# A longer opening run of zeros on TensorE, a later spread of norm's factors, and the first decays in two transfers and scans

## The chip, the cores and the metric

The kernel runs on one core of a Trainium2 chip. The metric is the device time of one execution in microseconds (us), and the median of several runs is compared. The engines are named as in the profile: PE (TensorE's matmuls; PEld are its weight loads), DVE (VectorE), ACT (ScalarE), POOL (GpSimd) and SP (SyncE, which here issues the DMA transfers). They run side by side and wait for each other by semaphores; each of them executes its own instructions strictly in the order of the program.

## What is computed

A gated linear attention over 4 batches x 8 heads x 768 steps with head size 48, and then a normed, gated feed-forward layer on its 3072 tokens of 384 features:

```python
state = alpha[:, :, t, :, None] * state + np.einsum('bhd,bhe->bhde', k[:, :, t], v[:, :, t])
y[:, :, t] = np.einsum('bhd,bhde->bhe', q[:, :, t], state)
...
rms = np.sqrt(np.mean(x * x, axis=-1, keepdims=True) + 1e-06)
xn = x / rms * rms_g
g = xn @ w_gate
silu = g * (1.0 / (1.0 + np.exp(-g)))
val = xn @ w_val
return (silu * val @ w_out).astype(np.float32)
```

The weights of the feed-forward layer come as 64-bit floats (w_gate and w_val 384 x 1536, w_out 1536 x 384).

## The kernel before, in words

**Chunks.** The 768 steps of each batch are cut into 6 chunks of 128 steps, all heads together, so that there are 24 chunks of 128 tokens. `attention(cc)` records the work of chunk cc. Chunks 0 to 3 are the first of their batches (`first`), have no state before them, and are computed with 32-bit matmuls; the others use 16-bit matmuls with each number split into a high and a low part.

**One first chunk, step by step.** SP loads the block `att` of the chunk: the decays (522 columns), then q and k (1024 columns). For chunks 0 and 1 these are two transfers (`cuts`), for the others one. DVE runs two scans over the 520 decay columns (`scan`, L661: cumulated products, four head pairs and two halves of the chunk in one row, each of these 8 segments starting anew), the first forward, the second backward from the reciprocals of the first one's ends (`turn`, L681). DVE multiplies q and k by the results (`mul_q` L698, `mul_k` L691). PE turns k (`k_across`, L893), computes the scores (`scores`, L778), DVE masks them (`masked32`, L794), and PE multiplies by v (`output32`, L804). The state goes through L908 on PE, two copies on ACT and L813 on PE. ACT squares the output (`square`, L960), POOL makes the norm's root, DVE multiplies by the root and by the factors rms_g (`scaled`, L974), and PE turns the result (`x_across` L981, with a low part by L995).

**The factors.** rms_g is loaded as one row (`load_rg`, L626), spread to all 128 partitions by a matmul with a row of ones, `unit` (`rg_wide`, L632), and copied back by ACT (`rg_take`, L635). `unit` lies in the same buffer as `junk`, the zeros that PE multiplies.

**The feed-forward layer.** Each of 18 weight tiles is loaded, folded and put together by ACT and DVE (`decode`: L536 on ACT, L541 and L544 on DVE, L502 on ACT, L552 on DVE). The chunks form groups of 4, 2, 2, 4, 4, 4 and 4. For each group and each of 12 weight tiles, PE runs two banks of 9 matmuls (L1149), ACT takes a silu of the first bank (L1160), DVE multiplies it with the second (L1166), and ACT and DVE split the product (L502, L1179). The second layer follows (L1219). In group 0, the first 5 weight tiles are run for chunks 0 and 1, and then for 2 and 3.

**What sets the order.** Nothing is issued by hand: `Plan.op` records each piece of work with its engine, a cost in us, what it depends on and which buffers it uses. `Plan.order` gives each piece a due time, from those of its users and from the tables `GAP`, `DUE`, `LATE` and `W_LATE`, and then lays the pieces out on a model of the five engines; the program's order on each engine is the result. Any cost or table entry that changes can so change the order of everything behind it. Where the model finds PE idle before its 45th microsecond, it fills in multiplications of a constant tile (`warm`, L1329), as many as fit at 0.24 us each.

**PE's start.** `warm_first` (L621) is PE's first piece: 14 matmuls of zeros, planned as 4.8 us.

```python
for _ in range(WARM_FIRST):
    nc.tensor.matmul(ps[:, :DM], junk[:, :P], junk, start=True, stop=True)
...
op("PE", 4.8, warm_first, [], [("mm", "warm")])
```

Of the kernel before, what the change touches and what calls it, by code (L numbers as in the profile page):

```python
# [8 lines left out]
F32 = mybir.dt.float32  # L9
# [37 lines left out]
GROUPS = [4, 2, 2, 4, 4, 4, 4]  # L47
EARLY = 5


# [10 lines left out]
COST = dict(  # L61
    scan=1.16, rec=0.18, kh=0.6, qh=0.33, kl=0.6, vl=0.47, ql=0.62, gd=0.12, sd=0.28, sl=0.27, mask=0.59,
    al=0.59, st=0.27, ss=0.12, x=0.46, xl=0.47, shift=0.53, rest=0.88, wl=0.87, ob=0.46,
# [12 lines left out]
PACE = [1.0, 1.0, 1.15, 1.18, 1.18, 1.18, 1.18]  # L76
GAP = [-15.7, 137.0, 36.9, 106.2, -22.7, -134.2, 399.9]
DUE = [
    -719.9, -428.4, 411.3, -551.6, 184.4, 443.0, 1038.8, 186.9, 211.3, 740.5, 1018.7, 654.7, 756.4,
    831.8, 770.0, 432.6, 1179.9, 1019.1, 1109.0, 512.2, 336.7, 338.7, 475.6, 483.2,  # L80
]
LATE = dict(
    a16=95.7, abs=95.5, add=-3.0, al=-37.8, cnt=239.3, dec=-143.8, gd=128.7, k16=-225.5, kb=-100.3,
    kh=211.5, kl=37.3, kp=-148.6, ld2=204.9, load=96.2, mask=-127.2, near=132.3, ob=-144.7,
    odd=-153.0, pow=73.9, q16=-96.0, qh=38.4, ql=-11.4, rec=52.2, rest=-69.8, rg=8.7, rgt=-201.8,
    rgw=-6.4, s16=44.3, sc=-125.2, sc32=-36.5, scan=303.9, sd=70.9, shift=-71.0, sl=-52.1, sq=109.6,
    st=-82.7, st0=-193.5, take=-59.8, u=-107.2, u32=-53.5, v=186.2, v16=124.3, vl=-14.9, wh=160.7,
    wid=-93.7, wl=-301.4, wl2=15.7, wneg=80.9, x=-230.4, x16=-36.5, x32=-16.4, xb=-7.0, xl=-43.5,
    xneg=126.0, xp=27.6, y32=-52.5, ys=-23.6, ys32=-78.8, ysw=-43.9, yv=-74.0, yvw=-116.3,
)  # L90
LATE_CHECK = 3
W_LATE = [
    -285.5, -492.0, -249.7, -250.4, -99.8, -149.6, -106.2, -73.2, 53.8, -132.7, 151.4, 126.2, 126.8,
    172.8, 286.5, 195.7, 182.1, 333.3,
]
WARM_UNTIL, WARM, WARM_FIRST = 45.0, 0.24, 14
CUTS = [0, 2, 4]
# [3 lines left out]
class Plan:  # L101
# [9 lines left out]
    def op(self, engine, cost, fn, deps=(), use=(), due=None, lock=False, kb=0, late=0.0, kind=None, tile=None):  # L111

        o = dict(e=engine, c=cost, fn=fn, d=[d for d in deps if d], u=tuple(use), due=due, lock=lock,
                 kb=kb, late=late, i=len(self.ops), n=[], k=kind, w=tile)
        for d in o["d"]:
            d["n"].append(o)
        for k in o["u"]:
            self.users[k] = self.users.get(k, 0) + 1
        self.ops.append(o)
        return o  # L120
# [224 lines left out]
def tile_attn_moe(  # L345
# [12 lines left out]
    nc = tc.nc  # L358
# [70 lines left out]


    tab = const.tile([1, 1], F32, name="tab")
    nc.gpsimd.memset(tab, 0.0)
    nc.scalar.activation(tab, tab, AF.Silu)
    rg = const.tile([P, DM], F32, name="rg")


    junk = const.tile([P, DM], mybir.dt.bfloat16, name="junk")
    unit = junk.bitcast(F32)[:1, :P]
    nc.vector.memset(junk, 0.0)
    nc.vector.memset(unit, 1.0)  # L440
    seed = const.tile([R, 2, NP, HC + 1], F32, name="seed")
# [71 lines left out]
    def add(engine, kind, *args, **kw):  # L513
        w = kw.get("tile")
        late = LATE.get(kind, 0.0) + (W_LATE[w] if w is not None else 0.0)
        return op(engine, COST[kind], *args, late=late, kind=kind, **kw)
# [105 lines left out]

    op("PE", 4.8, warm_first, [], [("mm", "warm")])

# [12 lines left out]
    def attention(cc):  # L637
# [18 lines left out]

        def scan(back, start):
            x, w = att_tile(cc)[:R, :o_a], decays()[:, o_f:]
            if back:
                x, w = [y[:R, 1 : o_a + 1][:, ::-1] for y in (att_tile(cc), decays())]  # L660
            nc.vector.tensor_tensor_scan(  # L661
                w, x, start.rearrange("r g p c -> r (g p c)"), 0.0, op0=ALU.mult, op1=ALU.add
            )
# [358 lines left out]
        att_k, w_k, at0, at1 = key("att"), key("w"), ("at", (cc, 0)), ("at", (cc, 1))  # L1022
        cuts = ((0, o_q), (o_q, AW)) if cc < 2 else ((0, AW),)
        la = [
# [6 lines left out]
        if cc == 0:  # L1031
            x = op("SP", 0.45, load_rg, kb=20, kind="rg", late=LATE.get("rg", 0.0))
            y = add("PE", "rgw", rg_wide, [x], [("mm", "rg")])
            tiles["rg"] = add("ACT", "rgt", rg_take, [y], [("mm", "rg")])
        before = state_ops.get(cc - NB, {})
        prev = state_ops.get(cc - 1, {})
        s1 = add("DVE", "scan", lambda: scan(False, seed), [la[0]], [att_k, w_k], lock=True)
        rec = add("DVE", "rec", turn, [s1, prev.get("s2")], [w_k])
# [10 lines left out]
        if first:  # L1049
# [4 lines left out]
            k_k, u_k = ("at", (cc, 4)), ("at", (cc, 2))  # L1054
            kt = add("PE", "kp", k_across, [kh], [key("kh"), k_k])
            kt = add("ACT", "kb", k_back, [kt], [key("kT"), k_k])
            y0 = add("PE", "y32", output32, [m, lv], [key("a16"), key("v"), key("y")])
# [25 lines left out]
        if cc in WIDE:  # L1083
            y_k = key("x32")
            y1 = add("ACT", "take", take, [y1], [key("y"), y_k])
            y1 = add("DVE", "add", add_up, [y1], [key("y"), y_k])
        sq = add("ACT", "sq", square, [y1], [y_k])
        rt = add("POOL", "pow", root, [sq], [key("ss")], lock=True)
# [422 lines left out]
```

## Time and profile before

| | before |
|---|---|
| median of 3 runs | 514.42 us (514.36, 514.42, 516.57) |
| the profiled execution | 516.7 us |
| its span, first to last instruction | 514.9 us |
| busy, share of the span | PE 98%, DVE 75%, PEld 59%, ACT 49%, POOL 6% |
| first gate matmul (L1149) on PE | 34.62 us after the start |
| last matmul's end | 510.9 us |
| moved from and to HBM | 52.03 MB read, 4.72 MB written |

How to read it: a row of the timeline gives the start, the duration, the engine, the line, the operation with its tiles and shapes, how many instructions were merged, and in brackets how long the engine idled before it and what ended that. "busy" of PE counts from the start of a matmul to its modelled end, so PE can be busy with work that is of no use to the result, such as multiplied zeros, or with work that runs slowly. In the table of stretches, each engine has its busy time and, in brackets, how many instructions; then come the granted clock, the share of the DMA engines' time, and GB/s.

### The profile page before, as it was taken

To read this page: it belongs to the slowest core of one execution; us is meant where nothing else is said; L and a number is where in the kernel's file an instruction comes from. 1 tells how busy PE (TensorE), PEld (TensorE's weight loads), DVE (VectorE), ACT (ScalarE), POOL (GpSimd) and SP (SyncE) were. 2 spreads that over 40 slices of the span, in tenths; PEclk is the share of its full clock that TensorE was granted. 3 is DMA by queue.
4 is the path that set the end of the run, shared out by engine and by line. 5 is a ranking of instruction groups with operands and counts; after the bars stand their busy time and mean duration, and the time that the engine had idled before them with its cause. 6 is when DMAs were issued, how large, how long until landed. Compare 5 with 4: busy or idle time off the path is not lost.

```text
span 514.9 us, 12237 instructions
## 1 busy us (share of the span) xinstructions
PE 507.0 (98%) x5004; PEld 302.5 (59%) x5004; DVE 387.0 (75%) x734; ACT 254.1 (49%) x669; POOL 30.0 (6%) x85
## 2 busy tenths in 40 slices
PE   8999999999999999999999999999999999999996
PEld 4687844668877886445556545556544456444453
DVE  6999999999999999969999998995364320233321
ACT  2578977635644762448644356754365310233300
POOL 4011000100000100001111000100010000000000
PEclk9999999999999999999999999999999999999999
DMA  8979866566542645321675824018862000000001
GB/s 295 297 229 263 226 220 212 154 124 165 114 96 94 130 116 138 96 81 32 142 229 149 179 89 168 17 32 277 287 203 77 1 17 31 17 0 1 0 31 36
DMA packets 64031, 65.19 MB, mean 127 GB/s; under 512 B 32993, under 2 KB 57570, under 8 KB 63970
## 3 DMA queue, kind: packets, MB, share of 16 engines
q1 hardware_dynamic: 63970, 64.36, 44.5%
q8 instruction: 40, 0.66, 0.5%
q14 instruction: 21, 0.17, 0.1%
HBM read 52.03 MB, written 4.72 MB: 110 GB/s over the span
## 4 chain that ended last, share of the span: by engine, by line
PE 87%; DVE 5%; issue 1%; ACT 1%; DVEq 0%; ACTq 0%
PE mm L1149 53%; PE mm_po L1219 25%; PE at L768 3%; PE y L856 2%; PE at L933 1%; PE y L835 1%; DVE w L661 1%; DVE wu_i L544 0%; DVE wg L552 0%; DVE wu_i L541 0%; DVE qp L698 0%; DVE k L705 0%; DVE kh L691 0%; ACT h L502 0%; DVE h L1166 0%
## 5 line engine op out<-in xcount | busy, mean ns | idle before, releaser
L1149 PE MATMUL mm<-xT,wg 128*128 128x512 f16 (+1 forms) x1602 | 287.5, 338 | 0.0
L1149 PEld LDWEIGHTS <-wg 128*128 128x128 f16 x1602 | 153.8, 98 | 120.0 <-issue 0.5
L1219 PE MATMUL mm_po<-wo,h 128*128 128x384 f16 x864 | 144.0, 326 | 0.0
L1219 PEld LDWEIGHTS <-h 128*128 128x128 f16 x864 | 83.2, 98 | 55.8 <-issue 1.0
L1166 DVE SCALAR_TENSOR_TENSOR h<-mm,sl 128x512 f32<-128x512 f32 (+1 forms) x89 | 51.6, 584 | 46.0 <-PE mm L1149 43.4
L502 ACT ACTIVATE h<-h 128x512 f16<-128x512 f32 (+1 forms) x89 | 48.6, 546 | 73.5 <-DVE h L1166 73.0
L1160 ACT ACTIVATE sl<-mm 128x512 f32<-128x512 f32 (+1 forms) x89 | 45.5, 511 | 49.1 <-PE mm L1149 48.0
L1179 DVE TENSOR_TENSOR h<-h,h 128x512 f16<-128x512 f32 (+1 forms) x89 | 51.5, 584 | 18.1 <-ACT h L502 18.1
L661 DVE TENSOR_TENSOR_SCAN w<-att,seed 112x520 f32<-112x520 f32 x48 | 59.4, 1238 | 2.5 <-DMA att<-att 1.8
L1230 DVE TENSOR_SCALAR ob<-mm_po 128x384 f32<-128x384 f32 x24 | 13.2, 553 | 34.3 <-PE mm_po L1219 34.2
L964 POOL TENSOR_TENSOR ss<-ssq,eps 128x1 f32<-128x1 f32 x24 | 10.2, 425 | 351.8 <-ACT junk L960 351.8
L883 ACT CAST a<-at 128x512 f16<-128x512 f32 x40 | 22.9, 584 | 15.6 <-DVE at L784 15.5
L784 DVE TENSOR_TENSOR at<-at,mask 128x512 f32<-128x512 f32 x40 | 26.2, 690 | 2.3 <-PE at L768 2.1
L886 DVE TENSOR_TENSOR a<-at,a 128x512 f16<-128x512 f32 x40 | 26.4, 681 | 0.0
L502 ACT ACTIVATE q<-qp 112x512 f16<-112x512 f32 x20 | 12.5, 627 | 18.1 <-DVE qp L698 17.0
L698 DVE TENSOR_TENSOR qp<-att,w 112x256 f32<-112x256 f32 x48 | 18.8, 419 | 0.1
L768 PEld LDWEIGHTS <-k 48*128 48x128 f16 x480 | 13.5, 94 | 6.6 <-issue 5.1
L768 PE MATMUL at<-q,k 48*128 48x128 f16 x480 | 17.1, 217 | 0.1
L502 ACT ACTIVATION_READ_ACCUMULATOR h<-h 128x1 f32 x89 | 16.7, 188 | 0.0
L691 DVE TENSOR_TENSOR kh<-att,w 112x512 f32<-112x512 f32 x24 | 16.4, 684 | 0.0
L684 ACT COPY dec<-w 112x8 f32<-112x8 f32 x24 | 4.9, 203 | 22.3 <-DVE w L661 22.1
L608 ACT ACTIVATE wu_c<-wu_c 128x768 f32<-128x768 f32 x12 | 10.0, 836 | 9.4 <-DVE wu_c L602 9.4
(134 smaller groups left out, 449.3 us busy)
## 6 DMA issues: line engine op xcount, KB each, us to landing
att<-att SPq DMA_DIRECT2D x22, 773.0 KB, 5.1
v<-vtok SPq DMA_DIRECT2D x24, 192.0 KB, 3.1
out_dram<-ob SPq DMA_DIRECT2D x24, 192.0 KB, 2.0
raw_c<-w_gate SPq DMA_DIRECT2D x12, 384.0 KB, 4.1
raw_c<-w_val SPq DMA_DIRECT2D x12, 384.0 KB, 5.0
raw_d<-w_out SPq DMA_DIRECT2D x6, 768.0 KB, 4.5
raw_i<-w_gate SPq DMA_DIRECT2D x11, 384.0 KB, 4.3
raw_i<-w_val SPq DMA_DIRECT2D x11, 384.0 KB, 5.0
```

Source lines behind the costliest of these rows:

```text
L502: nc.scalar.activation(dst, src, AF.Copy, scale=scale, accum_out=stat[:rows, col : col + 1])
L661: nc.vector.tensor_tensor_scan(w, x, start.rearrange("r g p c -> r (g p c)"), 0.0, op0=ALU.mult, op1=ALU.add)
L698: nc.vector.tensor_tensor(by_half(t["qp"])[:, g], q, w, op=ALU.mult)
L768: nc.tensor.matmul(t["sc"][j][:, p, :], t["k16"][r, x, p, :], t["q16"][r, y, p, :], start=m == 0, stop=m == 2,)
L784: nc.vector.tensor_tensor(t["sc"][j], t["sc"][j], mask.to_broadcast([P, NP, C]), op=ALU.mult)
L883: nc.scalar.copy(a_tile()[:, j, 0], t["sc"][j])
L886: nc.vector.tensor_tensor(a_tile()[:, j, 1], t["sc"][j], a_tile()[:, j, 0], op=ALU.subtract)
L1149: nc.tensor.matmul(ps[:, :n], wg[:, f, x, j, kk, :], xT[:, y, kk, cs], start=i == 0, stop=i == 3 * NK - 1,)
L1160: nc.scalar.activation(t["sl"][:, :n], t[0][:, :n], AF.Silu, scale=1.0 / (S_X * S_W))
L1166: nc.vector.scalar_tensor_tensor(t["h"][:, :n], t[1][:, :n], S_H / (S_X * S_W), t["sl"][:, :n], op0=ALU.mult, op1=ALU.mult,)
L1179: nc.vector.tensor_tensor(h16_of(g, f)[:, 1, cs], t["h"][:, :n], h16_of(g, f)[:, 0, cs], op=ALU.subtract)
L1219: nc.tensor.matmul(t[i][:, :DM], h16_of(g, f)[:, x, ts], wo[:, f // 2, y, f % 2, :], start=f == 0 and m == 0, stop=f == NF - 1 and m == 2,)
```

## The change

The diff without the new numbers of the planner's tables (`GAP`, `DUE`, `LATE` and `W_LATE` are all replaced, which moves work on every engine):

```diff
+HALVED = 1
...
-    scan=1.16, rec=0.18, kh=0.6, qh=0.33, kl=0.6, vl=0.47, ql=0.62, gd=0.12, sd=0.28, sl=0.27, mask=0.59,
+    scan=1.16, half=0.62, rec=0.18, kh=0.6, qh=0.33, kl=0.6, vl=0.47, ql=0.62, gd=0.12, sd=0.28, sl=0.27, mask=0.59,
...
-WARM_UNTIL, WARM, WARM_FIRST = 45.0, 0.24, 14
+WARM_UNTIL, WARM, WARM_FIRST, WARM_COST = 45.0, 0.24, 21, 7.9
...
+    junk = const.tile([P, DM], mybir.dt.bfloat16, name="junk")
+    nc.vector.memset(junk, 0.0)
     tab = const.tile([1, 1], F32, name="tab")
...
-    junk = const.tile([P, DM], mybir.dt.bfloat16, name="junk")
-    unit = junk.bitcast(F32)[:1, :P]
-    nc.vector.memset(junk, 0.0)
-    nc.vector.memset(unit, 1.0)
+    unit = const.tile([1, P], F32, name="unit")
+    nc.gpsimd.memset(unit, 1.0)
...
-    op("PE", 4.8, warm_first, [], [("mm", "warm")])
+    op("SP", 0.8, lambda: None, due=-1000.0)
+    op("PE", WARM_COST, warm_first, [], [("mm", "warm")])
...
-        def scan(back, start):
+        def scan(back, start, lo=0, hi=o_a):
...
             nc.vector.tensor_tensor_scan(
-                w, x, start.rearrange("r g p c -> r (g p c)"), 0.0, op0=ALU.mult, op1=ALU.add
+                w[:, lo:hi], x[:, lo:hi], start.rearrange("r g p c -> r (g p c)")[:, lo:hi], 0.0,
+                op0=ALU.mult, op1=ALU.add,
             )
...
-        cuts = ((0, o_q), (o_q, AW)) if cc < 2 else ((0, AW),)
+        at = [0] + ([SEG] if cc < HALVED else []) + ([o_q] if cc < 2 else []) + [AW]
+        cuts = list(zip(at, at[1:]))
...
-            y = add("PE", "rgw", rg_wide, [x], [("mm", "rg")])
-            tiles["rg"] = add("ACT", "rgt", rg_take, [y], [("mm", "rg")])
+            lrg = x
...
-        s1 = add("DVE", "scan", lambda: scan(False, seed), [la[0]], [att_k, w_k], lock=True)
+        if cc < HALVED:
+            s1 = None
+            for x, lo, hi in ((la[0], 0, SEG), (la[1], SEG, o_a)):
+                s1 = op("DVE", COST["half"], lambda lo=lo, hi=hi: scan(False, seed, lo, hi), [x, s1], [att_k, w_k],
+                        lock=True, late=LATE.get("scan", 0.0), kind="scan")
+        else:
+            s1 = add("DVE", "scan", lambda: scan(False, seed), [la[0]], [att_k, w_k], lock=True)
...
+            if cc == 0:
+                y = add("PE", "rgw", rg_wide, [lrg, kt, sc], [("mm", "rg")])
+                tiles["rg"] = add("ACT", "rgt", rg_take, [y], [("mm", "rg")])
...
-        sq = add("ACT", "sq", square, [y1], [y_k])
+        sq = add("ACT", "sq", square, [y1, tiles["rg"]], [y_k])
```

So there are four parts. The zeros of `junk` are the first instruction on DVE and `unit` has a tile of its own; PE multiplies zeros 21 times, planned as 7.9 us. `rg_wide` depends on chunk 0's turned k and scores, and the squares depend on the factors. Chunk 0's decay block comes in two transfers of 260 and 262 columns, with a forward scan for each. And the tables are new. The dummy piece on SP delays nothing on the chip: it has no instruction, and stands only in the planner's model.

What the new order looks like where it matters. First PE, from the last multiplied zeros to the first product with v; `at_0_4` is chunk 0's turned k, `at_0_0` its scores, `mm_rg` the spread factors, `warm` the planner's fillers. Before:

```order
L621 MATMUL mm_warm_150<-junk_91 128x384
L632 MATMUL mm_rg_188<-rg_90,junk_91 128x384
L1329 LDWEIGHTS minus_115
L1329 MATMUL warm_195<-minus_115 128x512
...
L893 MATMUL at_0_4_203<-one_118,kh_0_201 128x112 x4
L778 MATMUL at_0_0_212<-qp_0_193,kh_0_201 64x64 x2
...
L1329 MATMUL warm_235<-minus_115 128x512
...
L804 MATMUL y_0_243<-v_0_173,a16_0_240 64x48 x16
```

and now:

```order
L622 MATMUL mm_warm_151<-junk_87 128x384
L896 MATMUL at_0_4_210<-one_119,kh_0_202 128x112 x4
L781 MATMUL at_0_0_218<-qp_0_196,kh_0_202 64x64 x2
...
L634 MATMUL mm_rg_240<-rg_92,unit_93 128x384
L1341 LDWEIGHTS minus_116
L1341 MATMUL warm_245<-minus_116 128x512
L807 MATMUL y_0_251<-v_0_183,a16_0_243 64x48 x16
```

The spread of the factors and three fillers have left the place between the zeros and chunk 0's k; one filler stands before L804's successor L807 where four stood. In all, the fillers after the first burst fall from 20 to 4.

Next DVE, from chunk 1's second scan to chunk 2's scans and behind them (a scan is printed as SCALAR_TENSOR_TENSOR; `w_1` is chunk 1's decays, `a16_0` chunk 0's masked scores, `wu_i1` and `wg` a weight tile). Before:

```order
L661 SCALAR_TENSOR_TENSOR w_1_208<-att_1_169,seed2_98 112x520
L794 TENSOR_TENSOR a16_0_240<-at_0_0_212,near_101 128x256
L794 TENSOR_TENSOR a16_0_240<-at_0_1_213,near_101 128x256
L698 TENSOR_TENSOR qp_1_260<-att_1_169,w_1_208 112x4x64 x2
L691 TENSOR_TENSOR kh_1_263<-att_1_169,w_1_208 112x2x4x64
L661 SCALAR_TENSOR_TENSOR w_2_274<-att_2_171,seed_94 112x520
L681 RECIPROCAL seed2_98<-w_2_274 112x8
L661 SCALAR_TENSOR_TENSOR w_2_274<-att_2_171,seed2_98 112x520
L541 TENSOR_SCALAR wu_i1_309<-raw_i1_178 128x768
L698 TENSOR_TENSOR qp_2_329<-att_2_171,w_2_274 112x4x64
L544 SCALAR_TENSOR_TENSOR wu_i1_309<-raw_i1_178,wu_i1_309 128x768
```

and now:

```order
L663 SCALAR_TENSOR_TENSOR w_1_206<-att_1_178,seed2_99 112x520
L701 TENSOR_TENSOR qp_1_238<-att_1_178,w_1_206 112x4x64 x2
L797 TENSOR_TENSOR a16_0_243<-at_0_0_218,near_102 128x256
L797 TENSOR_TENSOR a16_0_243<-at_0_1_219,near_102 128x256
L694 TENSOR_TENSOR kh_1_249<-att_1_178,w_1_206 112x2x4x64
L663 SCALAR_TENSOR_TENSOR w_2_268<-att_2_186,seed_95 112x520
L684 RECIPROCAL seed2_99<-w_2_268 112x8
L663 SCALAR_TENSOR_TENSOR w_2_268<-att_2_186,seed2_99 112x520
L694 TENSOR_TENSOR kh_2_301<-att_2_186,w_2_268 112x2x4x64
L542 TENSOR_SCALAR wu_i1_313<-raw_i1_188 128x768
L701 TENSOR_TENSOR qp_2_316<-att_2_186,w_2_268 112x4x64 x2
L545 SCALAR_TENSOR_TENSOR wu_i1_313<-raw_i1_188,wu_i1_313 128x768
```

Chunk 1's q has moved ahead of chunk 0's masked scores, and chunk 2's k and all of its q ahead of the weight's second step. Chunk 2's scores are masked some way behind, before chunk 3's first scan and so before chunk 1's x; before, they were masked behind both.

Last ACT, ahead of the first silu (`sl_0_0_0`; `xT_0` is group 0's turned input, `raw_i3` a weight tile being folded, `k16_4` chunk 4's k). Before:

```order
L998 CAST xT_0_393<-mm_x_1_490 128x3x128
L536 ACTIVATE raw_i3_398<-raw_i3_398,t_add_134 128x768
L960 ACTIVATE junk_91,ssq_143<-y_3_508 128x384
L502 ACTIVATE k16_4_606,stat_138<-kh_4_568 112x512
L1160 ACTIVATE sl_0_0_0_608<-mm_0_0_0_0_581 128x256
```

and now:

```order
L1001 CAST xT_0_433<-mm_x_1_510 128x3x128
L503 ACTIVATE k16_4_571,stat_139<-kh_4_555 112x512
L963 ACTIVATE junk_87,ssq_144<-y_3_519 128x384
L503 ACTIVATE wg_147,stat_139<-wu_i2_550 128x768
L537 ACTIVATE raw_i3_421<-raw_i3_421,t_add_135 128x768
L1172 ACTIVATE sl_0_0_0_618<-mm_0_0_0_0_573 128x256
```

One more instruction, the high part of weight tile i2, stands between the last piece of chunk 1's input and the first silu, and the fold of i3 has moved behind it.

## Prediction before the run

> **What bounds the kernel now.** I read the page first, then who waited for whom on PE, then the span cut into stretches.
>
> ```profile
> span 514.9 us, 12237 instructions
> ...
> PE 507.0 (98%) x5004; PEld 302.5 (59%) x5004; DVE 387.0 (75%) x734; ACT 254.1 (49%) x669; POOL 30.0 (6%) x85
> ...
> PE 87%; DVE 5%; issue 1%; ACT 1%; DVEq 0%; ACTq 0%
> ```
> ```profile
> PE mm_warm L621 <- DVE seed L444: 1.9, 1, 1.9
> PE mm_x L981 <- DVE x L974: 1.2, 2, 0.8
> PE mm_x L995 <- ACT xT L989: 0.5, 1, 0.5
> ```
> ```profile
> 8.00:22.04 14.04, 13.21 (x181) 8.81 (x181) 11.70 (x20) 5.77 (x13) 1.05 (x2) 1.00 0.96 330
> 22.04:34.62 12.58, 12.49 (x245) 10.13 (x245) 12.39 (x22) 8.38 (x22) 0.88 (x2) 1.00 0.89 275
> 34.62:50.57 15.95, 15.03 (x233) 12.73 (x231) 15.85 (x32) 13.57 (x41) 2.09 (x4) 1.00 0.81 227
> 50.57:510.90 460.33, 460.14 (x4335) 268.34 (x4333) 341.50 (x653) 224.65 (x592) 20.79 (x45) 1.00 0.41 112
> ```
> Columns of the last fence: stretch, length, then busy time of PE, PEld, DVE, ACT and POOL. From 50.57 to 510.90 PE idles 0.2 us in 460; nothing there can be shortened by removing waits. The two later waits of PE (mm_x, 1.7 us in all) lie between 21 and 50.5. So the end is 510.9 minus whatever the first 50 us give up, and only there can the change act. DVE, 98% busy in both middle stretches, paces them.
>
> Busy is not useful, though. PE's first 22 us:
>
> ```profile
> 1.87 4.66 PE L621 MATMUL mm_warm<-junk 128*128 128x384 bf16 x14 [1.87 <-DVE seed L444]
> 6.46 1.64 PE L632 MATMUL mm_rg<-rg,junk 1*128 1x384 f32 x2
> 8.04 1.46 PE L1329 MATMUL warm<-minus 128*128 128x512 f16 x3
> 9.29 1.89 PE L893 MATMUL at<-one,kh 112*128 112x112 f32 x8
> 11.11 1.13 PE L778 MATMUL at<-qp,kh 48*64 48x64 f32 x32
> 12.18 1.89 PE L1329 MATMUL warm<-minus 128*128 128x512 f16 x4
> 14.00 1.27 PE L804 MATMUL y<-v,a 64*64 64x48 f32 x30
> ...
> 15.72 1.15 PE L893 MATMUL at<-one,kh 112*128 112x112 f32 x8
> ...
> 18.23 2.98 PE L1329 MATMUL warm<-minus 128*128 128x512 f16 x13
> 22.04 0.71 PE L981 MATMUL mm_x<-one,x 128*128 128x128 f32 x4 [0.83 <-DVE x L974]
> ```
> ```profile
> 14.00:14.45 0.45, 0.45 (x8) 0.45 (x10) 1.00 1.10 355
> 14.45:14.90 0.45, 0.45 (x21) 0.45 (x20) 1.00 1.23 413
> ```
> The same L893 group takes 1.89 us at 9.3 and 1.15 at 15.7. The second fence is L804 alone: 8 matmuls in 0.45 us, then 21 in the next 0.45. TensorE doubled its rate at about 14.45 us, although the granted-clock column says 1.00 throughout. The 4.6 us of zeros from 1.87 to 6.46 had not done it, nor the light matmuls (one row, or 48 of 128) from 6.46 to 12.
>
> **The change, part by part.** DVE carries the path:
>
> ```profile
> 0.92 0.22 DVE L439 MEMSET junk<- 128x192 uint32 x1 [0.92 <-PEq L1500]
> ...
> 3.66 1.24 DVE L661 TENSOR_TENSOR_SCAN w<-att,seed 112x520 f32<-112x520 f32 x1 [1.82 <-DMA att<-att]
> 5.01 0.21 DVE L681 RECIPROCAL seed<-w 112x8 f32<-112x8 f32 x1
> ...
> 7.29 0.69 DVE L691 TENSOR_TENSOR kh<-att,w 112x512 f32<-112x512 f32 x1
> ...
> 9.58 1.24 DVE L661 TENSOR_TENSOR_SCAN w<-att,seed 112x520 f32<-112x520 f32 x1
> 12.35 0.76 DVE L794 TENSOR_TENSOR a<-at,near 128x256 f32<-128x256 f32 x2 [1.53 <-PE at L778]
> 13.02 0.75 DVE L698 TENSOR_TENSOR qp<-att,w 112x256 f32<-112x256 f32 x2
> ...
> 14.46 1.24 DVE L661 TENSOR_TENSOR_SCAN w<-att,seed 112x520 f32<-112x520 f32 x1
> ...
> 18.47 0.96 DVE L544 SCALAR_TENSOR_TENSOR wu_i<-raw_i,wu_i 128x768 int32<-128x768 int32 x1 [0.46 <-ACT raw_i L536]
> ```
> *Halved transfer and scan.* These rows price the transfers (SP's issues, then the landings):
>
> ```profile
> 0.81 0.87 SPq L423 DMA_DIRECT2D att<-att  x2
> 1.73 0.32 SPq L626 DMA_DIRECT2D rg<-rms_g  x1
> ...
> att<-att SPq DMA_DIRECT2D x2, 261.0 KB, 3.9
> ```
> 261 KB at the 330 GB/s of the stretch from 8 us is 0.79 us; half the bytes land up to 0.4 earlier, or not earlier at all if the delay is not the bytes. With 3.3 as the start, the halves take 0.62 each (1.24/2) and the second ends near 4.55 instead of 4.90: **-0.35**, bounds -0.4 and +0.1 (one more instruction). The price: the 512 KB of q and k for chunk 0 are issued behind one more transfer and rg's, 0.43 + 0.37 = 0.8 later. DVE took them at 6.6 without a wait, so they landed at most 5.35 after their issue at 1.25; that is 7.4 now at worst, against a need at 6.25: up to +1.1. By bytes (773 KB, 2.3 us at 330 GB/s, from 3.66 - 0.79 = 2.9) they land at 5.2, so I take 0, the nearer row.
>
> *Burst without a break.* Junk's zeros are ready at 1.14, no longer behind the later memset of unit, so PE starts near 1.2. 21 matmuls at the cold 0.32 us (14 from 1.87 to 6.46, less the wait behind the last) end at 7.9 or sooner, as chunk 0's kh ends at 7.98 - 0.35 = 7.63 (7.29 + 0.69 before). The three fillers and rg that stood ahead of L893 are gone, so L893 starts at 7.9 instead of 9.29 and, at the doubled rate, takes 1.15 (the row at 15.72) and L778 0.6 (half of 1.13): scores at 9.65 instead of 12.3. DVE leaves the second scan at 10.5 and now does qp of chunk 1 first (the order rows above), so the 1.53 us wait goes: **-1.53**, bounds -1.53 and 0 (burst in vain). Next late is then DVE's own chain: chunk 2's scan at 12.6 instead of 14.46.
>
> *rg later.* Its matmul stands behind the scores, PE idle there until L794 anyway (9.6 to 11.6); its copy on ACT comes before the first square. Behind the copy on ACT stand instructions that wait for DVE's scan of chunk 2 until 13.9. The first user, x of chunk 0, is at about 18.9: 0. If that cover were gone it would cost its 1.6 us.
>
> *SP's queue.* Chunk 1's q and k now go ahead of v and of chunk 2's block. By bytes at 330 GB/s from 2.9, chunks 0 and 1 (1546 KB) are in by 7.6, v and chunk 2 (965 KB) by 10.5; DVE needs them at 10.5 and 12.6: 0. If a wait came of it, it would end with the bytes, under 0.5.
>
> *DVE's wait on ACT at 18.47.* ACT's fold of the first weight comes about 2 us earlier with PE's second L893, DVE only 1.9: **-0.46**, bounds -0.46 and 0.
>
> Sum for DVE: -2.34. Its work is only reordered (chunk 2's two L794 forward, a weight's shift back).
>
> *From there to the first gate matmul:*
>
> ```profile
> 29.24 0.60 DVE L974 SCALAR_TENSOR_TENSOR x<-y,ss,rg 128x384 f32<-128x384 f32 x1
> ...
> 34.21 1.03 ACT L536 ACTIVATE raw_i<-raw_i,t_add 128x768 f32<-128x768 int8 x1
> 34.62 5.09 PE L1149 MATMUL mm<-xT,wg 128*128 128x256 f16 x45
> ...
> 36.19 0.40 ACT L1160 ACTIVATE sl<-mm 128x256 f32<-128x256 f32 x1
> ...
> 48.57 0.94 PE L981 MATMUL mm_x<-one,x 128*128 128x128 f32 x6 [0.35 <-DVE x L974]
> ...
> 50.41 0.32 PE L995 MATMUL mm_x<-xT,minus 128*128 128x384 f16 x1 [0.50 <-ACT xT L989]
> ```
> Chunk 1's x starts at 29.24 - 2.34 + 0.75 (chunk 2's L794 now ahead of it) = 27.65. From there to L1149 it took 5.38, of which chunk 2's L893 and L778 (1.15 + 0.6) are now done before: 31.3, and near 32 with PE's wait for chunk 3's L794 behind that x. That is 2.6 earlier. But on ACT the first silu (L1160) now stands behind k's split, a square, a weight's split and a fold, about 3.3 us from 32.2, so it comes at 35.8, hardly earlier than 36.19. The fourth group waits there for its bank, some 0.7 us: part of the 2.6 is given back, and DVE's 2.34 stays the measure. The waits at 48.57 and 50.41 (0.35 + 0.5) get a weight tile's two gate groups more as cover in the new order: -0.85 to 0, I take half, **-0.4**, since nothing shows which of the two goes. Total -2.7. The profiled execution was 516.7 (514.9 and 1.8 around it): 516.7 - 2.7 = **514.0**.
>
> **How that stands to the median.** The runs shown are 514.36, 514.42 and 516.57: two values 2.2 apart. The profiled 516.7 lies with the upper one. What would make the lower one is in the rows: had the rate doubled within the first burst, the wait of 1.53 and the 0.46 would be gone, 2.0 together. I conclude that the kernel has early and late clocks, and that the profile shows a late one. Then the change makes every run an early one, and against the median of 514.42 only -0.35 and some of the 0.4 remain.
>
> [...]
>
> **Rivals.**
> 1. *The profile is typical and the profiler adds 2 us.* Then the whole 2.7 comes off the median: 511.7. For it: one of three runs at 516.57 may be noise. Against: 514.4 + 2.2 meets both upper values.
> 2. *The clock falls back* (slower). Only 4 fillers are left behind the burst where 20 stood, and PE has gaps near 10, 17.5 and 23. If light matmuls don't hold the rate, L893 and L778 are cold again on DVE's path from chunk 1 on. A late clock to about 14 us is the profile's 516.7; held to the first gate matmuls it adds some 0.7 per L893 (1.89 - 1.15) for three chunks, 2.2: 518. It decides if PE drops before 16 us. Against: from 22.04 to 34.62 the trace has light matmuls alone and no drop, and a 0.83 us gap just before.
> 3. *The change doesn't do what it says*: the burst is in vain, so the 1.53 and the 0.46 stay: 516.7 - 0.35 - 0.4 = 515.95, or with q and k late (+1.1) 516 to 517 all told. For it: a first burst in vain is in the profile. Against: the new one is 2.1 us longer and no light matmul follows it before kh.
>
> **How the numbers follow.** Forecast 0.70 (513.4 to 515.4: below with the whole 0.85, above with the late q and k), rival 1 0.15, rival 2 0.07, rival 3 0.08. The range 511.6 to 515.4 holds the forecast and over half of rival 1. About 0.5% (2.6 us) is what a measurement can tell from no change: faster than 511.85 is a little over half of rival 1, 0.09; slower than 517.0 is most of rival 2, 0.05; the rest 0.86.
>
> **What would show it.** L621 x21 from about 1.2 without a gap and L893 right behind at under 8; 1.0 us for it, not 1.8. Two scans of 112x260, the reciprocal near 4.65. No wait before DVE's first L794, chunk 2's scan near 12.6. First L1149 near 32, its fourth group waiting for ACT. From 52 on PE without idle. Wrong I am if PE idles after 52, if L893 is cold, or if the late clock is not what makes 516.6.

## The result and the profile after

The changed kernel takes 518.41 us (median of 13 runs, 515.1 to 519.65), against 514.42 us for the kernel before, timed beside it (13 runs, 514.22 to 516.57). The medians lie 4.0 us apart. The ratio is 1.0063, with a 95% interval of 1.0043 to 1.0084, so the change is slower. The forecast was 514.0 with a range of 511.6 to 515.4.

The page of the changed kernel (its profiled execution took 518.55 us):

```profile
span 516.7 us, 12224 instructions
...
PE 509.0 (99%) x4995; PEld 305.9 (59%) x4995; DVE 387.6 (75%) x734; ACT 254.8 (49%) x669; POOL 38.5 (7%) x86
...
PEclk9589999999999999999999999999999999999999
...
PE 84%; DVE 9%; DMA 2%; ACT 1%; issue 1%; SPq 0%; DVEq 0%; ACTq 0%
```

PE is busier than before (509.0 us instead of 507.0) with nine matmuls fewer, and DVE's share of the chain that ended last rose from 5% to 9%. The row PEclk has a 5 and an 8 in its second and third of 40 slices (12.9 us each). The table of stretches, cut where the granted clock changes, with the columns of the prediction's table (length, busy time of PE, PEld, DVE, ACT and POOL, granted clock, DMA share, GB/s):

```profile
9.52:12.93 3.41, 2.41 (x46) 1.45 (x46) 3.29 (x7) 0.53 (x2) 0.00 (x0) 1.00 1.06 366
12.93:29.99 17.06, 17.06 (x202) 13.88 (x198) 13.50 (x23) 7.80 (x19) 2.13 (x4) 0.50 0.81 288
29.99:36.19 6.20, 6.20 (x131) 5.04 (x129) 5.07 (x11) 4.11 (x10) 1.31 (x1) 1.00 0.49 163
36.19:516.70 480.51, 475.45 (x4568) 281.02 (x4564) 358.81 (x683) 239.96 (x634) 29.27 (x49) 1.00 0.43 115
```

From 12.93 to 29.99 us TensorE has half its clock. PE is busy all that time, and DVE, which was busy for 3.29 of the 3.41 us before, does 13.50 us of work in 17.06. PE's timeline (rows as in the prediction) shows what stood before the fall, and what the fall does to the same groups:

```profile
1.19 5.98 PE L622 MATMUL mm_warm<-junk 128*128 128x384 bf16 x21 [1.19 <-DVE junk L434]
7.61 1.12 PE L896 MATMUL at<-one,kh 112*128 112x112 f32 x8 [0.44 <-DVE kh L694]
8.65 0.70 PE L781 MATMUL at<-qp,kh 48*64 48x64 f32 x32
9.28 0.91 PE L634 MATMUL mm_rg<-rg,unit 1*128 1x384 f32 x2
10.12 0.39 PE L1341 MATMUL warm<-minus 128*128 128x512 f16 x1
11.50 1.29 PE L807 MATMUL y<-v,a 64*64 64x48 f32 x30 [0.99 <-DVE a L797]
...
13.47 2.05 PE L896 MATMUL at<-one,kh 112*128 112x112 f32 x8
...
20.21 1.13 PE L781 MATMUL at<-qp,kh 48*64 48x64 f32 x32
...
30.86 1.15 PE L896 MATMUL at<-one,kh 112*128 112x112 f32 x8
...
36.19 3.12 PE L1161 MATMUL mm<-xT,wg 128*128 128x256 f16 x27
```

The first rows are as forecast: the zeros run without a break, the keys (L896, L893 before) start at 7.61 and take 1.12 us, the factors (L634) come behind the scores. Then come one row of weights for 0.91 us, one filler, 0.99 us without work, and products of 64 rows (L807); at 12.93 the rate halves. Keys take 2.05 us behind the fall (at 13.47), and 1.15 once the rate is back (at 30.86). The first gate multiplication (L1161, L1149 before) starts at 36.19; 32 was forecast, and 34.62 stood in the profile before. Where DVE pays for it, in its timeline:

```profile
24.04 1.24 DVE L663 TENSOR_TENSOR_SCAN w<-att,seed 112x520 f32<-112x520 f32 x1
28.26 0.76 DVE L701 TENSOR_TENSOR qp<-att,w 112x256 f32<-112x256 f32 x2 [2.97 <-PE y L816]
...
32.67 0.76 DVE L797 TENSOR_TENSOR a<-at,near 128x256 f32<-128x256 f32 x2 [0.72 <-PE at L781]
```

DVE, which paced this part before, waits 2.97 us for L816, products of 48 rows and 48 columns that PE, at half rate, reaches only then. Over all 13 runs the mean granted clock of the span lies between .979 and .990 (.983 in the profiled one), so the rate fell in every one. The runs with the lower granted clock are the slower ones: 515.1 and 515.2 at .989 and .990, 519.2 to 519.65 at .979 and .980.

### The profile page after: what moved, and what is told of

The parts are those of the page before. It is cut to its first block, busy times and chain, and to the rows that moved or that the text cites. A ratio compares the mean times of both kernels' runs of the same rounds, so it can differ in the third digit from the quotient of the medians.

```text
span 516.7 us, 12224 instructions
## 1 busy us (share of the span) xinstructions
PE 509.0 (99%) x4995; PEld 305.9 (59%) x4995; DVE 387.6 (75%) x734; ACT 254.8 (49%) x669; POOL 38.5 (7%) x86
## 4 chain that ended last, share of the span: by engine, by line
PE 84%; DVE 9%; DMA 2%; ACT 1%; issue 1%; SPq 0%; DVEq 0%; ACTq 0%
PE mm L1161 46%; PE mm_po L1231 24%; PE at L771 3%; PE y L859 2%; PE at L936 1%; DMA raw_i<-w_val 1%; DMA kT<-k 1%; PE y L838 1%; DVE wu_o L545 1%; PE y L807 1%; DVE wo L553 1%; PE at L896 1%; DVE wu_i L545 1%; PE at L911 1%; DVE h L1178 1%
## 5 line engine op out<-in xcount | busy, mean ns | idle before, releaser
L1161 PE MATMUL mm<-xT,wg 128*128 128x512 f16 (+1 forms) x1602 | 287.9, 339 | 0.6 <-ACT xT L1001 0.6
L1161 PEld LDWEIGHTS <-wg 128*128 128x128 f16 x1602 | 153.8, 98 | 120.6 <-issue 0.8
L1231 PE MATMUL mm_po<-wo,h 128*128 128x384 f16 x864 | 144.3, 327 | 0.4 <-DVE ob L1242 0.4
L1231 PEld LDWEIGHTS <-h 128*128 128x128 f16 x864 | 83.2, 98 | 56.2 <-issue 1.4
L663 DVE TENSOR_TENSOR_SCAN w<-att,seed 112x520 f32<-112x520 f32 (+1 forms) x49 | 59.5, 1216 | 1.7 <-DMA att<-att 1.2
L967 POOL TENSOR_TENSOR ss<-ssq,eps 128x1 f32<-128x1 f32 x24 | 15.5, 648 | 364.0 <-ACT junk L963 364.0
L701 DVE TENSOR_TENSOR qp<-att,w 112x256 f32<-112x256 f32 x48 | 18.5, 420 | 3.2 <-PE y L816 3.1
L503 ACT ACTIVATE q<-qp 112x512 f16<-112x512 f32 x20 | 12.6, 628 | 16.3 <-DVE qp L701 14.2
L503 ACT ACTIVATE k<-kh 112x512 f16<-112x512 f32 x20 | 12.4, 622 | 11.4 <-DVE kh L694 9.2
L968 POOL TENSOR_TENSOR ss<-ss,mhalf 128x1 f32<-128x1 f32 x24 | 16.4, 685 | 1.9
```

What stands on the lines that cost most here:

```text
L503: nc.scalar.activation(dst, src, AF.Copy, scale=scale, accum_out=stat[:rows, col : col + 1])
L663: nc.vector.tensor_tensor_scan(w[:, lo:hi], x[:, lo:hi], start.rearrange("r g p c -> r (g p c)")[:, lo:hi], 0.0, op0=ALU.mult, op1=ALU.add,)
L701: nc.vector.tensor_tensor(by_half(t["qp"])[:, g], q, w, op=ALU.mult)
L1161: nc.tensor.matmul(ps[:, :n], wg[:, f, x, j, kk, :], xT[:, y, kk, cs], start=i == 0, stop=i == 3 * NK - 1,)
L1231: nc.tensor.matmul(t[i][:, :DM], h16_of(g, f)[:, x, ts], wo[:, f // 2, y, f % 2, :], start=f == 0 and m == 0, stop=f == NF - 1 and m == 2,)
```

## Theories and experiments

**Theory 1:** the rate falls because the fillers that kept TensorE's clock on are gone: where the kernel before had 3, 4 and 13 of them, the changed one has four single ones. **Theory 2:** the new order costs the time by itself. **Theory 3:** the prediction's reading of before (early and late clocks) is wrong, so that the profile of before hid something. The first four kernels tell these apart; the next six ask where the fillers must stand, what must be in them, and what each part of the change is worth.

### The kernel before once more

No edit.

> The kernel before, once more, for a second profile of it. Clock theory: most executions are near 514.4, and in such an execution the TensorE rate doubles inside the first burst of zeros, before 6.5 us, so that L893 takes 1.15 us at its first place too, DVE doesn't wait 1.5 us before its first L794, and the first L1149 stands near 32.7 instead of 34.6. Rival (the profiler adds 2 us, nothing to do with the clock): a profile like the first one, L893 cold at 9.3, first L1149 at 34.6, and 514.4 outside the profiler.

Measured: 514.39 us (514.26 to 515.72, 8 runs), ratio 0.9987 (0.9968 to 1.0007); profiled 514.41. PE's timeline:

```profile
6.46 1.21 PE L632 MATMUL mm_rg<-rg,junk 1*128 1x384 f32 x2
7.60 0.82 PE L1329 MATMUL warm<-minus 128*128 128x512 f16 x3
8.26 1.04 PE L893 MATMUL at<-one,kh 112*128 112x112 f32 x8
...
19.84 0.94 PE L981 MATMUL mm_x<-one,x 128*128 128x128 f32 x6 [1.36 <-DVE x L974]
```

The same program as in the profile before, but here the first keys take 1.04 us at 8.26 instead of 1.89 at 9.29: the rate doubled during L632 (1.21 us instead of 1.64), a little later than expected. The first gate matmul stands at 32.40 (32.7 expected). That is the early clock that the prediction inferred, 2.3 us below the late one of 516.7, and the profiler adds nothing. Theory 3 falls.

### The changed kernel with its fillers back

`fills` gives the number of fillers at each of the four places at which the planner had put one.

```diff
+    fills = [6, 6, 1, 1]
...
     def warm(slot, n):
+        n = fills.pop(0)
```

> The changed kernel in its own order; only the first two fillers grow from 1 to 6 multiplications each (before the first product with v, and after chunk 1's scores), where PE has idle time or light work. Clock theory (the rate falls to half near 12.9 us because PE does little there, and all of the loss is that): the granted clock is over 0.995, no stretch below 1.00 after the burst, first L1149 near 32, time 510.5 to 512.5, which would beat both kernels. Order theory (the new order itself is slow, the clock only goes along): 515 or more, clock or not.

Measured: 513.75 us (513.61 to 515.26, 10 runs), ratio 0.9984 (0.9970 to 0.9999); profiled 513.74. All else is the changed kernel, in its order. The clock did what the clock theory said (.996 to 1.0 in all ten runs), but the 510.5 to 512.5 expected of it was too low. The table of stretches:

```profile
9.52:12.93 3.41, 3.41 (x49) 1.85 (x50) 3.29 (x7) 0.56 (x2) 0.00 (x0) 1.00 1.02 361
12.93:31.83 18.90, 17.27 (x338) 13.68 (x334) 18.32 (x33) 11.80 (x29) 2.90 (x4) 1.00 0.90 316
31.83:511.90 480.07, 475.22 (x4568) 280.91 (x4564) 358.77 (x683) 239.71 (x634) 28.85 (x49) 1.00 0.43 116
```

and, from its timelines, the rows for which the prediction gave times:

```profile
3.06 1.34 DVE L663 TENSOR_TENSOR_SCAN w<-att,seed 112x260 f32<-112x260 f32 x2 [1.23 <-DMA att<-att]
4.50 0.21 DVE L684 RECIPROCAL seed<-w 112x8 f32<-112x8 f32 x1
...
12.50 1.24 DVE L663 TENSOR_TENSOR_SCAN w<-att,seed 112x520 f32<-112x520 f32 x1
```
```profile
7.65 1.12 PE L896 MATMUL at<-one,kh 112*128 112x112 f32 x8
...
31.83 3.12 PE L1161 MATMUL mm<-xT,wg 128*128 128x256 f16 x27
34.89 0.66 PE L911 MATMUL at<-v,kT 64*64 64x48 f32 x16
35.48 1.92 PE L1161 MATMUL mm<-xT,wg 128*128 128x256 f16 x16
```

The clock stays on, DVE has 18.32 us of work in 18.90, and the first gate matmul starts 4.36 us earlier than in the changed kernel. Behind it both take nearly the same, 480.07 and 480.51 us. Ten added fillers, which compute nothing that is used, are the only difference between the two kernels, and make the 4.66 us between the medians. Theory 2 falls: the new order, once its clock is kept, is no slower than the old one.

### The kernel before without its fillers

```diff
+    fills = [3, 1, 1]
...
+        n = fills.pop(0)
```

> The kernel before in its own order; only its second and third fillers shrink from 4 and 13 multiplications to 1 each. Clock theory: without them the rate is at half for a stretch in most executions (doubled late, or fallen back), clock below 0.99 or a late first doubling, 516 to 520 and as scattered as the changed kernel. Order theory: nothing happens, 514.4, since the fillers stand in idle time of PE.

Measured: 521.26 us (518.29 to 528.03, 4 runs), ratio 1.0164 (1.0089 to 1.0239); 516 to 520 was expected. Three of the four runs lie above every run of the changed kernel, so the old order without 15 of its 20 fillers is no better off. The stretch ahead of the fall, and PE's row behind it:

```profile
15.57:18.98 3.41, 0.23 (x1) 0.00 (x0) 3.35 (x7) 2.50 (x7) 1.56 (x2) 1.00 0.99 381
```
```profile
19.75 1.65 PE L981 MATMUL mm_x<-one,x 128*128 128x128 f32 x6 [3.95 <-DVE x L974]
```

Here it is the wait of PE before L981: 1.36 us behind 13 fillers in the second profile of the kernel before, 3.95 without them. After a stretch with 0.23 us of work the granted clock is 0.50 (from 20 to 25 us), and L981 takes 1.65 us instead of 0.94. So the fillers of before carried weight, in a place where PE had nothing else to do. (In two of the four runs, 521.02 and 528.03, the granted clock reads 1.0. The column also read 1.00 before the first doubling in the profile before, so they may be runs in which the rate came on late; no trace of them exists, and why one took 528.03 stays open.)

### The burst alone

The kernel before, with junk's zeros written first, `unit` in a tile of its own, and 21 zeros without a break; the planner is left at the old order, and its first filler place has 1 instead of 3.

```diff
-WARM_UNTIL, WARM, WARM_FIRST = 45.0, 0.24, 14
+WARM_UNTIL, WARM, WARM_FIRST = 45.0, 0.24, 21
...
+    junk = const.tile([P, DM], mybir.dt.bfloat16, name="junk")
+    nc.vector.memset(junk, 0.0)
...
+    unit = const.tile([1, P], F32, name="unit")
+    nc.gpsimd.memset(unit, 1.0)
...
+    fills = [1, 4, 13]
```

> The kernel before with the burst alone: zeros are DVE's first instruction, the row of ones has a tile of its own, 21 multiplications instead of 14, and 1 filler instead of 3 right behind rg's matmul so that chunk 0's k isn't pushed back; fillers 4 and 13 and the whole order stay. Clock theory: every execution is an early one, 514.0 to 514.7, none near 516.6, clock 1.00. Rival (the burst itself brings the fall): clock below 0.99 and 516 or more.

Measured: 514.37 us (514.29 to 514.48, 10 runs), ratio 0.9985 (0.9971 to 0.9999). All ten runs lie where the early ones of before lie. None is at 515.6 or 516.5, where 19 of the 84 runs of before lie that were timed beside these kernels, and 9 of the 25 that were timed beside this one. If each run had that last chance (0.36), ten without one would come about once in ninety times. The traces show the same: in those with the longer burst the 21 zeros take 5.04 to 6.47 us, and at the prediction's cold 0.32 us each they would take 6.7; chunk 0's keys behind them take 1.04 to 1.12 us, not 1.89. So the rate doubled within the burst each time. The longer burst takes nothing from the median, as forecast.

### Which fillers

The first place is behind chunk 0's scores, the second behind chunk 1's. (The expectations of these two runs count the chunks from 1 here.)

```diff
+    fills = [6, 1, 1, 1]
```

> The changed kernel with its first place of filler multiplications (behind chunk 1's keys, near 10 us) raised from 1 to 6, the other three places left at 1. Theory 1 (the rate falls after a stretch of about 3.4 us in which TensorE idles or does little; the cost of the change is this fall at 12.93 us): the five fillers more fill the 0.5 to 1 us of idle time in the stretch from 9.5 to 12.9 us, so the fall at 12.93 us goes; the next thin stretch (13 to 20 us, filled by six of the second place in the kernel with both raised) may still fall, one or two steps of 3.4 us later. If it holds: 513.7 to 514.5; if it falls near 16 to 20 us: 515 to 518, with the rate back near 30 us. Theory 2 (the time comes from the new order, not from the clock): 518, as the changed kernel. Theory 3 (it is the sum of fillers that counts, whatever the place): 515 to 517 in this kernel and in the next alike.

Measured: 514.91 us (513.63 to 518.03, 10 runs), in three heaps: two runs at 513.6 to 513.7, four at 514.8 to 514.9, four at 517.1 to 518.0. In the profiled execution (514.81) the fall at 12.93 is gone (the granted clock is 1.00 from 12 to 15 us), as theory 1 said. The median lies between the two ranges expected, and the rate falls not at 16 to 20 us, as expected, but here:

```profile
24.68:28.09 3.41, 2.26 (x54) 1.96 (x56) 3.22 (x6) 1.45 (x4) 0.83 (x2) 1.00 0.67 203
28.09:31.50 3.41, 3.41 (x49) 2.98 (x41) 3.05 (x9) 1.59 (x5) 0.00 (x0) 0.50 0.66 239
```

It stays off for 3.41 us. The stretch before it holds a wait of PE for chunk 3's keys (1.15 us). The four slowest runs have a lower granted clock (.985 to .989), so their rate was off for longer; where, no trace shows. The fastest, 513.63, has .995, lower than the .996 of the middle heap: it seems that a fall can also cost nothing.

```diff
+    fills = [1, 6, 1, 1]
```

> The changed kernel with its second place of fillers (behind chunk 2's keys) raised from 1 to 6 and the first left at 1. Theory 1 (a thin stretch of 3.4 us makes the rate fall): nothing before 12.9 us differs from the changed kernel, so the rate still falls near 12.9 us in most runs; six fillers at half rate are about 2.5 us of dense work, which may bring the rate back one or more steps sooner than 30 us, so 515 to 518.5, and slower than the kernel with the first place raised. Theory 2 (order): 518. Theory 3 (the sum of fillers): the same as with the first place raised, within 0.5 us.

Measured: 516.15 us (514.73 to 516.84, 10 runs), granted clock .988 to .992 in all, as theory 1 said. Up to the second place this is the changed kernel, and the rate falls as there (at 11.36); then it comes back early. The stretches ahead of the fall and of the return, and PE's timeline:

```profile
7.95:11.36 3.41, 2.65 (x43) 1.63 (x42) 3.31 (x6) 1.22 (x3) 0.00 (x0) 1.00 0.99 378
...
18.18:21.60 3.42, 3.42 (x36) 1.84 (x30) 3.36 (x7) 2.35 (x6) 1.21 (x2) 0.50 0.88 285
```
```profile
18.94 2.74 PE L1344 MATMUL warm<-minus 128*128 128x512 f16 x6
21.48 1.10 PE L896 MATMUL at<-one,kh 112*128 112x112 f32 x8
```

Six full fillers at half rate last 2.74 us, and behind them the rate doubles, at 21.60; the changed kernel, with one filler there, waited until 29.99. The place matters, not only the sum: with the same number of fillers the two kernels differ by 1.2 us in their medians.

### Busy or at work?

The five added fillers of each six multiply one row of weights instead of 128. PE is as long busy; what they compute is used by nobody in either form.

```diff
-        for _ in range(n):
+        for i in range(n):
+            k = 1 if i else P
             nc.tensor.matmul(
-                ps.rearrange("p (o c) -> p o c", o=4), minus,
-                minus.rearrange("p (o c) -> p o c", o=1).to_broadcast([P, 4, P]),
+                ps.rearrange("p (o c) -> p o c", o=4), minus[:k],
+                minus[:k].rearrange("p (o c) -> p o c", o=1).to_broadcast([k, 4, P]),
```

> The changed kernel with six fillers at the first and at the second place, where it had one; but of each six, five multiply one row of weights instead of 128 (1 x 512 columns, so TensorE is as long busy and does next to nothing). What they compute is used by nobody in either form. Theory 1a (idle time in the stretch of 3.4 us makes the rate fall): as with full fillers, 513.75. Theory 1b (what counts is how much of the array works, so one row is as good as a pause): the rate falls near 12 to 13 us as in the changed kernel, though at one of the later steps it may come back, 516 to 520. Values of both kinds would mean a threshold near this case.

Measured: 521.82 us (519.44 to 522.95, 4 runs), granted clock .976 to .982 in all: the fall of theory 1b, and more time than its 516 to 520.

```profile
8.93:12.35 3.42, 3.42 (x56) 1.77 (x56) 3.32 (x8) 1.22 (x3) 0.00 (x0) 1.00 1.02 367
12.35:32.83 20.48, 20.48 (x231) 15.55 (x228) 13.89 (x23) 7.76 (x19) 1.80 (x3) 0.50 0.72 250
```

The table of stretches, cut at the fall and the return, has PE busy for all 3.42 us ahead of the fall: not one pause, and the rate falls all the same. With fillers of 128 rows in the same places none of ten runs was above 515.3. So this fall needed no pause: little work in each matmul was enough, and the matmuls of one row held the rate no better than none. The kernel is even slower than the changed one: at half rate the six fillers ahead of chunk 2's keys take 2.85 us, where its one takes 0.61.

### The decays in halves

The kernel with the burst alone, plus chunk 0's decays in two transfers and two forward scans, in the old order:

```diff
+        at = (lo, SEG, hi) if cc == 0 and lo == 0 else (lo, hi)
+        for lo, hi in zip(at, at[1:]):
...
+            for lo, hi in ((0, SEG), (SEG, o_a)) if cc == 0 and not back else ((0, o_a),):
...
```

> The kernel before with the burst alone, and chunk 0's decays in two transfers and two forward scans (the order of the rest as before). By the term of the sum: 0.35 us less than the burst alone (514.37), so 514.0. Against it: if what is gained ahead of the first keys is lost at a later wait that is not tied to the scan, 514.3 to 514.5; if the clock rather than the scan sets the time in this order too, a spread of values above 515.

Measured: 514.53 us (513.88 to 514.73, 11 runs), ratio 0.9997 (0.9988 to 1.0006): not the 514.0 expected. In the trace the reciprocal comes 0.22 us earlier than with the burst alone (4.69 against 4.91), but the keys come later, at 8.66 against 8.10. First DVE's row, then PE's, and last PE's with the burst alone:

```profile
6.97 0.68 DVE L695 TENSOR_TENSOR kh<-att,w 112x512 f32<-112x512 f32 x1
```
```profile
1.20 6.47 PE L623 MATMUL mm_warm<-junk 128*128 128x384 bf16 x21 [1.20 <-DVE junk L434]
7.60 0.91 PE L634 MATMUL mm_rg<-rg,unit 1*128 1x384 f32 x2
8.44 0.39 PE L1336 MATMUL warm<-minus 128*128 128x512 f16 x1
8.66 1.04 PE L897 MATMUL at<-one,kh 112*128 112x112 f32 x8
```
```profile
1.19 5.91 PE L621 MATMUL mm_warm<-junk 128*128 128x384 bf16 x21 [1.19 <-DVE junk L432]
...
8.10 1.04 PE L893 MATMUL at<-one,kh 112*128 112x112 f32 x8
```

kh is ready at 7.65 (6.97 + 0.68), and PE still has the factors and a filler ahead of it, so nothing is won at the keys. That they come later here than with the burst alone is no work of the halves: the 21 zeros took 6.47 us in this execution and 5.91 in the other, because the rate doubled later within them. DVE has no added wait, and its lead is down to 0.13 at chunk 2's scan (12.60 against 12.73); these two executions differ by 0.2 us (514.26 and 514.46). Why the eleven runs spread over 513.9 to 514.7 and their median shows no gain stays open.

So the halves were measured in the new order as well: the kernel with fillers 6, 6, 1, 1, its order kept, with one transfer and one forward scan.

```diff
+        if cc == 0 and lo == SEG:
+            return
+        hi = o_q if cc == 0 and lo == 0 else hi
         nc.sync.dma_start(att_tile(cc)[:, lo:hi], att[src(cc), :, lo:hi])
...
+            if (lo, hi) == (0, SEG):
+                return
+            lo = 0
```

> The kernel with six fillers at the first and at the second place, its order kept word for word, but chunk 0's decays in one transfer and one forward scan again, as before the change. By the term of the sum (0.35 us on VectorE's chain, which paces this stretch): 513.75 + 0.35 = 514.1. If the halves are worth nothing behind the burst (the zeros end at about 7.6 us, when the keys are ready only 0.2 us earlier): 513.7 to 513.8. In the trace: the reciprocal near 4.9 instead of 4.50, the first gate multiplication near 32.2 instead of 31.83.

Measured: 514.33 us (514.03 to 515.59, 10 runs), ratio 1.0003 (0.9993 to 1.0012): 0.58 more than with the halves, where 0.35 was expected. DVE's timeline:

```profile
3.62 1.24 DVE L669 TENSOR_TENSOR_SCAN w<-att,seed 112x520 f32<-112x520 f32 x1 [1.79 <-DMA att<-att]
4.97 0.21 DVE L690 RECIPROCAL seed<-w 112x8 f32<-112x8 f32 x1
```

The first half lands 0.56 us earlier than the whole (3.06 against 3.62), the reciprocal comes 0.47 earlier, the first gate matmul 0.43 (31.83 against 32.26), and the span is 0.6 shorter (511.9 against 512.5).

### A denser filling

The kernel with 6, 6, 1, 1 had three of ten runs at 514.4 to 515.3. Six multiplications of 448 columns were put into the wait of 1.16 us ahead of chunk 3's keys.

```diff
+            for _ in range(6 if cc == 3 else 0):
+                nc.tensor.matmul(
+                    t["kp"], minus, minus[:, :R].rearrange("p (o c) -> p o c", o=1).to_broadcast([P, NP, R]),
+                    start=True, stop=True,
+                )
```

> The changed kernel with both places raised to 6, and six dense multiplications of 448 columns into kp's bank ahead of chunk 3's keys, where TensorE idled 1.16 us in the kernel with both places raised. Theory 1: the two or three runs at 514.4 to 515.3 that the kernel with both places raised had (granted clock .996 to .997) were falls in a thin stretch near 26 us; they go, and all runs lie within 513.5 to 513.9, median 513.65; the six cost nothing, since TensorE waits there, or up to 0.3 where they reach past the wait. Against it: if those runs had another thin stretch (near 18 or 23 us), the spread stays as it was.

Measured: 513.72 us (513.59 to 514.86, 11 runs), ratio 0.9982 (0.9973 to 0.9992). Ten runs lie within 513.59 and 513.97, one at 514.86, where 513.5 to 513.9 was expected of all. No granted clock is under .998 (the 514.86 has 1.0, so it isn't a fall that the records show; its cause is open). The six cost nothing that the medians show (513.72 against 513.75) and take out the two runs at .996 and .997; with so few runs this is a hint. It has the lowest median of all, 0.18% below before by the ratio; the kernel with 6, 6, 1, 1 alone is no different from it within this spread.

## Why the prediction was wrong, point by point

**The step that failed** is the last one of the reading of the median, "the change makes every run an early one", with the dismissal of rival 2 at a chance of 0.07. An early start is what the burst gives; the step took it for granted that a rate once doubled stays. The rival had the mechanism, its place ("only 4 fillers are left behind the burst where 20 stood") and its condition ("if PE drops before 16 us"; it dropped at 12.93). It was dropped for one stretch of the trace: light matmuls alone from 22.04 to 34.62, behind a gap of 0.83 us, and no drop there. Beside the runs, that stretch was not light: it holds L561, L564, L981 and L893 with 112 or 128 rows, while the stretch that fell holds one row (L634), one filler, 64 rows (L807) and 0.99 us of nothing. (The same loose word stands for 6.46 to 12 us, where three fillers of 128 rows and L893 with 112 ran as well.) How busy PE was doesn't tell the two cases apart: in the profile before it was busy for 2.65 us of the 3.41 from 21.28 (two steps of 3.41 behind the doubling) to 24.69, gap included, and the rate held; with 1, 6, 1, 1 it fell behind the same 2.65 of 3.41. The fillers were counted as cost and cover, never as the thing that keeps the clock, though the profile before showed 20 of them in just the gaps of PE.

**The price of the rival** came out near, 518 against a median of 518.41 (515.1 to 519.65), but by another path, so that is luck in part. It was 516.7 for the late clock and 0.7 us more for the keys of three chunks. That makes 518.9; 518 comes only with the 0.35 and the 0.4 of the other terms taken off, which the prediction doesn't say. In the trace the start is early, and only two groups of keys are slow (2.05 us at 13.47, 1.89 at 18.39; chunk 3's has the rate back). What costs the time is that all of PE's work from 12.93 to 29.99 us takes longer, so that PE, not DVE, sets the pace there: the first gate matmul comes 4.36 us later than with the fillers, and DVE waits 2.97 us at L701, where it doesn't wait with them.

**The rest of the sum held**, as the kernel with fillers shows. Its profiled execution is at 513.74 against the 516.7 of before: -3.0 where -2.7 was worked out. That this is so near is luck in part, since the burst and the halves brought more than their terms and the waits at 48.57 and 50.41 nothing.

- *Burst*: no break, the keys at 7.65 (7.9 forecast) for 1.12 us (1.15), no wait of DVE at L797 and none for ACT behind it; chunk 2's scan at 12.50 (12.6). Right. That 21 zeros would double the rate within them was an estimate, and no run had shown it: in the profile before, 14 of them (4.66 us) had not. With the longer burst the traces show 21 zeros in 5.04 to 6.47 us and the keys at the doubled rate behind them. The late and the early execution of before lie 2.3 us apart, where 1.53 and 0.46 made 2.0. Against the early runs the burst is worth nothing, as said.
- *Halved transfer and scan*: -0.35 forecast, -0.58 measured between medians. Right mechanism in the new order, too small: the first half landed 0.56 us earlier, more than the 0.4 that its bytes gave as a bound. In the old order the median shows none of it. The later q and k cost nothing, as taken: DVE's L701 starts at 6.14 without a wait.
- *Factors later*: 0 by itself was forecast. No kernel here moves the factors alone, so this isn't shown. It may be what lets the halves gain at the keys in the new order and not in the old, which the prediction didn't see.
- *First gate matmul*: near 32 forecast, 31.83, and chunk 1's x ahead of it at 27.63 (27.65). But the fourth group's wait of 0.7 for ACT didn't come: L1161 goes on at 35.48 right behind L911.
- *Waits at 48.57 and 50.41*: half of 0.85 was to go. With the burst alone as the start (514.37), the new order with its fillers and whole decays is at 514.33: the order as such is worth 0.04 between medians, not 0.4, though three of those ten runs lie at 515.2 to 515.6. The trace of the kernel with fillers shows a reason: both waits are gone, but two others have come, 0.58 us before a gate matmul and 0.3 before L1231, in the second layer. (PE idle behind 52 us was one of the prediction's own signs of being wrong.) First PE's timeline, then its waits:

```profile
49.49 10.74 PE L1161 MATMUL mm<-xT,wg 128*128 128x256 f16 x93 [0.58 <-ACT xT L1001]
```
```profile
PE mm_po L1231 <- DVE ob L1242: 0.3, 1, 0.3
```

- *Early and late clocks in the kernel before, and no time added by the profiler*: right, as its second profile shows. Rival 1 falls.

**The ledger** in medians: burst alone 514.37; the new order, its fillers at 6, 6, 1, 1 and the decays whole 514.33; with the halves 513.75; the fillers as the planner left them 518.41. The change gains 0.6 and pays 4.7, and 4.36 of that is lost ahead of the first gate matmul.

## What to carry to other kernels

Work that computes nothing can be what a kernel's clock rests on: before taking fillers out, or letting a planner decide how many fit, look at what dense work is left on TensorE around them. Here ten full fillers were worth 4.66 us between the medians (518.41 and 513.75); with one row in place of 128 in those ten the median was 521.82, no better than without them. Where the clock's moment differs from run to run, as in the two profiles of the kernel before (516.7 and 514.41 us), a single profile shows one case of several, so read every run's granted clock before the sum is made.

## What the runs showed of the hardware

- **The rate changed in steps of one length.** It was off for 17.06, 20.48 and 3.41 us in the rows above: 5, 6 and 1 times 3.41. (With 1, 6, 1, 1 it was off from 11.36 to 21.60, 3 times.) The moment differs from run to run: the kernel before doubled its rate at 14.45 us in one profile and during L632 (from 6.46, for 1.21 us) in the other, and in the run without 15 of its 20 fillers it did so within the 14 zeros, which take 4.13 us there instead of 4.66, with L632 at 0.91 behind them. The runs of the kernel with 6, 1, 1, 1 lie in three heaps, and only one of them has a trace; why the moment differs was not shown.
- **A fall needed no long pause.** The rate fell behind 3.41 us with 2.41 us of work in them (the changed kernel), 2.65 (1, 6, 1, 1) or 2.26 (6, 1, 1, 1), so with 1.15 us of pause at most, and behind 3.42 us with no pause at all but little in each matmul (the thin fillers). Nor was a thin stretch enough by itself: the 2.65 of 3.41 us of the profile before did not make it fall.
- **Being busy didn't bring it back at once.** At half rate PE was busy 17.06 of 17.06 us in the changed kernel, mostly with matmuls of 48 to 112 rows, before the rate returned. In the kernel with 1, 6, 1, 1 it returned behind the stretch with the six full fillers. In the changed kernel and in the one with thin fillers it returned during L565 (29.99) and L562 (32.83), a weight's matmuls of 128 rows; an earlier L562 in the same traces had not brought it back (at 25.54 and 28.80). So where the border between light and dense lies was not measured.
- **The granted clock didn't tell all.** The column reads 1.00 before the first doubling (8 to 14.45 us of the profile before, where the keys take 1.89 us, against 1.15 at 15.72). So the late start is seen in the durations only; the fall is seen in both, 0.50 in the column and 2.05 us for the keys of the changed kernel.
